# Two decode attentions in one kernel: the keys and values of the windowed one (A) loaded for all 16 heads at once, ahead of the other one's (B's) head pairs

## The chip, the cores and the metric

One NeuronCore of a Trainium2 chip runs the whole program. The metric is the device time of one execution in microseconds (us). Matmuls run on the tensor engine (PE; its weight loads are shown as PEld), elementwise work and reductions on the vector engine (DVE), exponentials on the scalar engine (ACT), set-up work on GpSimd (POOL), and loads are issued from the sync engine (SP) and carried out by 16 DMA engines.

## The reference

Two grouped-query attentions with one query token each. Every one has 32 query heads on 16 key heads of 128 elements, a cache of 8,192 tokens, a query projection and an output projection. A looks at the last W = 2,048 tokens only, B at all 8,192.

```python
Hq, Hkv, Sk, Dh, D = 32, 16, 8192, 128, 576
q = (x @ wq).reshape(1, 1, 32, 128).transpose(0, 2, 1, 3)
k = repeat(k_cache[:, :, Sk - W:, :], 2, axis=1)      # A: W = 2048; B: the whole cache
v = repeat(v_cache[:, :, Sk - W:, :], 2, axis=1)
scores = einsum("bhqd,bhkd->bhqk", q, k) * Dh ** -0.5
o = einsum("bhqk,bhkd->bhqd", softmax(scores), v)
out = o.transpose(0, 2, 1, 3).reshape(1, 1, 4096) @ wo
return concatenate([out_A, out_B], axis=-1)
```

All tensors are bfloat16. K and V are 4.2 MB per pair of B's heads, 8.4 MB for all of A's heads; wq and wo are 4.7 MB each. Together some 102.8 MB are read once.

## The kernel before

The program is written out by hand: each engine has a list of operations, and `op` and `load` put semaphore waits in front of an operation for the names in its `deps`. Within an engine the order of the list is the order of execution.

**Loads.** All big loads are issued from SP, in one list, into one buffer `ring` of 72 K elements (144 KB) per partition. `place` gives each load the next stretch, goes back to the start when it does not fit, and makes the load wait until the last use of what it overwrites (the names in `uses`). The order is wq of A and B, then for each of the eight head pairs p: K of B (4 MB, one row of 32 KB for each of 128 partitions), K of A (1 MB, two rows of 4 KB for each partition, one for each head), V of B, V of A; then wo of A, and wo of B in six pieces that get smaller.

**Queries.** x is spread over the partitions (`xd`, `xT`, `xr`), multiplied with wq in 16 units of 512 columns (`qmm`), copied out by ACT and DVE in turn (`qe`), transposed (`qT`), and laid into mostly zero weight blocks `zb` (B) and `za` (A), so that one 128-column matmul puts the two queries' scores of one slab of keys on their own rows of the score bank.

**A head pair.** K comes in slabs of 2,048 elements per partition: eight of B and two of A (`NI` = 10). DVE transposes a slab (L335, names `T`), PE multiplies it in four matmuls (L345, `S`), all ten into one bank. Then one softmax for B and A of this pair: maximum (`max`, L354), across partitions by a matmul (`mT`), per head on one partition (`mrB`, `mrA`, `mxB`, `mxA`), back to all partitions (`bc`, `nb`), exponential with row sums on ACT (`exp`, L380), two DVE transposes (`PT`, L384). The V matmuls follow (L393 for B, L400 for A, names `V`), the results are copied out (`xo0` on ACT, `xo1` on DVE, L409) and folded per head by PE (`OB` L414, `OA` L421). Scores alternate between two banks, three transposed slabs are kept (`NKT`).

**End.** Sums are inverted and applied (`lsel`, `L`, `rl`, `on`), the 32 heads are brought into wo's order (`oq`, `pm`, `oP`), and PE runs the output projection (L457, `F0.0`, then `F1.0` to `F1.5` as the pieces of wo land).

POOL makes an identity at the start and sets `zb`, `za`, `pts` to zero; DVE sets `vb` to zero and derives small selection tables from the identity.

Of the kernel before, what the change touches and what calls it, by code (L numbers as in the profile page):

```python
# [4 lines left out]
BF16 = mybir.dt.bfloat16  # L5
F32 = mybir.dt.float32
# [5 lines left out]
HQ = 32  # L12
# [9 lines left out]
NB = 2 * SK // 128 * DH // SLAB  # L22
NI = NB + 2
W0 = 2 * (NB - 1)
ZW = 128 + W0
RING = 72 * 1024
# [80 lines left out]
def bass_concat_heads__sliding_block_cached__gqa_block_cached__decode_kernel(nc, A_x, A_k_cache, A_v_cache, A_wq, A_wo,  # L107
# [5 lines left out]

    ring = nc.alloc_sbuf_tensor("ring", [128, RING], BF16)
# [12 lines left out]
    za = nc.alloc_sbuf_tensor("za", [128, NP, 2, 4, 128], BF16)  # L127
    mx = nc.alloc_sbuf_tensor("mx", [128, 2], F32)
    mr = nc.alloc_sbuf_tensor("mr", [128, 8], F32)
    mexp = nc.alloc_sbuf_tensor("mexp", [128, 128], F32)  # L130
    nb = nc.alloc_sbuf_tensor("nb", [128, 2], F32)
# [4 lines left out]
    cls = nc.alloc_sbuf_tensor("cls", [128, 8], F32)  # L136
    selb = nc.alloc_sbuf_tensor("selb", [128, 16], F32)
    sela = nc.alloc_sbuf_tensor("sela", [128, 4], F32)
    par = nc.alloc_sbuf_tensor("par", [128, 2], F32)
    lsel = nc.alloc_sbuf_tensor("lsel", [128, NP, 8], F32)  # L140
    rl = nc.alloc_sbuf_tensor("rl", [128, NP * 8], F32)
# [60 lines left out]
    kv_at = {}  # L202
    for p in range(NP):
        for kind, c in (("K", ks), ("V", vs)):
            use = "T%d.%d" if kind == "K" else "V%d.%d"
            src = c[1][0, 2 * p:2 * p + 2, :, :].rearrange("h (q t) d -> (h q) (t d)", q=64)
            kv_at[kind, p, 0] = place(NB * SLAB, [use % (p, NB - 1)],
                                      lambda e, t, src=src: e.dma_start(t, src), "%sB%d" % (kind, p))
            src = c[0][0, 2 * p:2 * p + 2, SK - W_A:SK, :].rearrange("h (q t) d -> q h (t d)", q=128)
            kv_at[kind, p, 1] = place(2 * SLAB, [use % (p, NI - 1)],  # L210
                                      lambda e, t, src=src: e.dma_start(t.rearrange("q (h n) -> q h n", h=2), src),
                                      "%sA%d" % (kind, p))
# [23 lines left out]
    op("pool", lambda e: e.memset(zb[:], 0.0), name="zb0")  # L236
    op("pool", lambda e: e.memset(za[:], 0.0), name="za0")
    op("pool", lambda e: e.memset(mexp[:], 0.0), name="mexp0")
    op("pool", lambda e: e.memset(onesf[:], 1.0), name="ones")
    op("pool", lambda e: e.memset(pts[:], 0.0), name="pts0")  # L240
# [3 lines left out]
    for b in range(2):  # L244
        op("dve", lambda e, b=b: e.memset(vb[b][:, :], 0.0), name="vb0.%d" % b)
# [3 lines left out]
    for h in range(2):  # L249
        op("dve", lambda e, h=h: e.tensor_reduce(  # L250
            cls[:, 2 * h:2 * h + 2], view(identf, 128, 64 * h, [[1, 2], [32, 2], [2, NB]]), AX.XY, ALU.add),
            deps=["identf"], name="clsB%d" % h)
    op("dve", lambda e: e.tensor_reduce(cls[:, 4:8], view(identf, 128, 2 * NB, [[1, 4], [32, 4]]), AX.X, ALU.add),
       deps=["identf"], name="clsA")
    op("dve", lambda e: e.tensor_reduce(selb[:], view(identf, 128, 0, [[1, 16], [32, 4]]), AX.X, ALU.add),
       deps=["identf"], name="selb")
    op("dve", lambda e: e.tensor_reduce(sela[:], view(identf, 128, 0, [[4, 2], [1, 2], [32, 4], [2, 2]]), AX.XY, ALU.add),
       deps=["identf"], name="sela")
# [3 lines left out]
    for P in range(2):  # L262
# [14 lines left out]
        for c in range(2):  # L277
            op("dve", lambda e, P=P, c=c: e.tensor_scalar(  # L278
                xrep[:, P, 4 + c, :], banks[2 * P + 1][:, 0:128], par[:, c:c + 1], None, ALU.mult),
                deps=["xT%d.4" % P, "par%d" % c], name="xr%d.%d" % (P, 1 + c))  # L280
    XR = ["xr%d.%d" % (P, c) for P in range(2) for c in range(3)]

    KT = NKT * SLAB
    for P in range(2):
        for n in range(8):
# [17 lines left out]
            else:  # L303
# [4 lines left out]
                deps=["qe%d" % u] + (["z0.%d" % i for i in range(8)] if P else []), name="qT%d" % u)  # L308
        srcs = [[512, NP], [64, 2], [1, 2], [128, 2]]
        for b in range(4):  # L310
            if P == 1:
                op("dve", lambda e, b=b: e.tensor_copy(
                    view(zb, NP * 4 * ZW, 32 * b + W0, [[4 * ZW, NP], [2 * ZW, 2], [ZW, 2], [1, 2]], 32, 32 * b),
                    view(ktb, KT, b // 2 * 256, srcs, 32, 32 * b)),
                    deps=["qT%d" % u for u in range(8, 16)] + ["zb0"], name="z1.%d" % b)
            else:
                for h in range(2):
                    op("dve", lambda e, b=b, h=h: e.tensor_copy(
                        view(za, NP * 1024, h * 512 + 32 * b + 2 * (NB + h),
                             [[1024, NP], [256, 2], [128, 2], [1, 2]], 32, 32 * b),  # L320
                        view(ktb, KT, h * 256, srcs, 32, 32 * b)),
                        deps=["qT%d" % u for u in range(8)] + ["za0"], name="z0.%d" % (2 * b + h))
    Z = ["z0.%d" % i for i in range(8)] + ["z1.%d" % i for i in range(4)]


    def unit(kind, p, s):
        return "%s%s%d" % (kind, "BA"[s // NB], p)

    for p in range(NP):
        for s in range(NI):  # L330
            k = p * NI + s
            kt = ktb[:, (k % NKT) * SLAB:(k % NKT + 1) * SLAB]
            deps = [unit("K", p, s)]
            deps += ["S%d" % (k - NKT)] if k >= NKT else Z
            op("dve", lambda e, p=p, s=s, kt=kt: e.transpose(kt.bitcast(I32), slab("K", p, s).bitcast(I32)),  # L335
               deps=deps, name="T%d.%d" % (p, s))

            def mm(e, p=p, s=s, k=k):
                for c in range(2):
                    for v in range(2):  # L340
                        if s < NB:
                            lhsT = zb[:, p, 2 * c + v, W0 - 2 * s:W0 - 2 * s + 128]
                        else:
                            lhsT = za[:, p, s - NB, 2 * c + v, :]
                        ins = e.matmul(sb[p % 2][:, :], lhsT=lhsT,  # L345
                                       rhs=view(ktb, KT, (k % NKT) * SLAB + 64 * c + v, [[128, 16], [2, 32]]),
                                       start=(s == 0 and c == 0 and v == 0), stop=(s == NI - 1 and c == 1 and v == 1))
                return ins
            deps = ["T%d.%d" % (p, s)]
            if s == 0:  # L350
                deps += ["exp%d" % (p - 2), "max%d" % (p - 2)] if p >= 2 else Z + ["qe%d" % u for u in range(16)]
            op("pe", mm, deps=deps, name="S%d" % k)

        op("dve", lambda e, p=p: e.tensor_reduce(mx[:, 0:1], sb[p % 2][:, :], AX.X, ALU.max),  # L354
           deps=["S%d" % (p * NI + NI - 1)] + (["mT%d" % (p - 1)] if p else []), name="max%d" % p)
        op("pe", lambda e: e.matmul(mb[0:1, 0:128], lhsT=mx[:, 0:1], rhs=identf[:, :], start=True, stop=True),  # L356
           deps=["max%d" % p, "identf"] + (["mrA%d" % (p - 1), "mrB1.%d" % (p - 1), "nb%d" % (p - 1)] if p else []),
           name="mT%d" % p)
        deps = ["mT%d" % p] + (["bc%d" % (p - 1)] if p else ["mexp0"])
        for h in range(2):  # L360
            op("dve", lambda e, h=h: e.tensor_reduce(
                mr[0:1, 2 * h:2 * h + 2], view(mb, 512, 64 * h, [[1, 2], [32, 2], [2, NB]], parts=1), AX.XY, ALU.max),
                deps=deps + (["mxB%d.%d" % (h, p - 1)] if p else []), name="mrB%d.%d" % (h, p))
        op("dve", lambda e: e.tensor_reduce(
            mr[0:1, 4:8], view(mb, 512, 2 * NB, [[1, 4], [32, 4]], parts=1), AX.X, ALU.max),
            deps=deps + (["mxA%d" % (p - 1)] if p else []), name="mrA%d" % p)
        for h in range(2):
            op("dve", lambda e, h=h: e.tensor_scalar(
                view(mexp, 128, 64 * h, [[32, 2], [2, NB], [1, 2]], parts=1),
                view(mr, 8, 2 * h, [[0, 2], [0, NB], [1, 2]], parts=1), -SCALE, None, ALU.mult),  # L370
                deps=["mrB%d.%d" % (h, p)], name="mxB%d.%d" % (h, p))
        op("dve", lambda e: e.tensor_scalar(
            view(mexp, 128, 2 * NB, [[32, 4], [1, 4]], parts=1),
            view(mr, 8, 4, [[0, 4], [1, 4]], parts=1), -SCALE, None, ALU.mult),
            deps=["mrA%d" % p], name="mxA%d" % p)
        op("pe", lambda e: e.matmul(mb[:, 128:129], lhsT=mexp[0:1, :], rhs=onesf[0:1, 0:1], start=True, stop=True),
           deps=["mxA%d" % p, "mxB0.%d" % p, "mxB1.%d" % p, "ones"], name="bc%d" % p)
# [5 lines left out]
        for h in range(2):  # L383
            op("dve", lambda e, h=h: e.transpose(  # L384
                view(pts, 1024, 2 * h, [[4, 16], [64, 16], [1, 2]], 64, 64 * h), psb[64 * h:64 * h + 64, :]),
               deps=["exp%d" % p] + (["V%d.%d" % (p - 1, NI - 1)] if p else ["pts0"]), name="PT%d.%d" % (h, p))

        for s in range(NI):
            def mm(e, p=p, s=s):
                src = slab("V", p, s)  # L390
                if s < NB:
                    for j in range(4):
                        ins = e.matmul(vb[0][32 * j:32 * j + 16, :],  # L393
                                       lhsT=view(pts, 1024, 64 * s + 16 * j, [[1, 16]]),
                                       rhs=src[:, 512 * j:512 * j + 512], start=(s == 0), stop=(s == NB - 1))
                else:
                    h = s - NB
                    for t in range(8):
                        j = t % 4
                        ins = e.matmul(vb[1][32 * j:32 * j + 8, 256 * h:256 * h + 256],  # L400
# [104 lines left out]
```

## Time and profile before

Three runs took 249.95, 250.19 and 251.74 us; the median is 250.19. One execution was profiled.

| what | value |
|---|---|
| the profiled execution: its time, its span | 250.0 us, 248.2 us |
| bytes read, mean rate over the span | 102.76 MB, 414 GB/s |
| DMA engines, share of the span in the SP queue's packets | 97.9% |
| PE busy, DVE busy, ACT busy, POOL busy | 73%, 62%, 7%, 5% |
| granted PE clock, mean | 0.82 |
| DVE transposes of K slabs (L335) | 80, 92.4 us, 1,213 ns each |
| score matmuls (L345) | 320, 90.3 us |
| loads of K and V of B: size, issue to landing | 4,096 KB, 27 us |
| loads of K and V of A: size, issue to landing | 1,024 KB, 27 to 29 us |

The span runs from the first to the last instruction of the profile; the 1.8 us around it belong to the time. The "busy" of an engine is the time in which it has an instruction in work. A DMA packet is one contiguous row as a DMA engine moves it. "Issue to landing" is how long after SP issued a load its data were complete, waiting behind earlier loads included.

### The profile page before, as it was taken

The numbers are of one execution on the slowest core, as the hardware profiler recorded it, in microseconds if no ns is written. First come the engines' busy times: TensorE is split into PE (matmuls) and PEld (weight loads), VectorE is DVE, ScalarE is ACT, GpSimd is POOL, SyncE is SP. The second block draws the span as 40 slices with busy tenths as digits, with TensorE's granted clock in tenths as the row PEclk, the third lists the DMA queues.
The fourth block names the chain that finished last, engine by engine and source line by source line (L and its number), as shares of the span: only waits on it lengthen the run. The fifth ranks groups of instructions, "written<-read, shape, count | busy, mean of one in ns | idle before, by whom it ended". The sixth has DMA issues, their size and how long they took to land.

```text
span 248.2 us, 2581 instructions
## 1 busy us (share of the span) xinstructions
PE 181.7 (73%) x1085; PEld 80.7 (33%) x1085; DVE 153.1 (62%) x228; ACT 18.1 (7%) x36; POOL 13.4 (5%) x15
## 2 busy tenths in 40 slices
PE   0039994957995799379746984998489757975795
PEld 0013441313631342143224321732153124322552
DVE  8963779952885298439734873487349725972300
ACT  2001220010001000100010001000100010001000
POOL 8920000000000000000000000000000000000000
PEclk9999999795589599877987597569677957895769
DMA  7999999999999999999999999999999999999992
GB/s 264 418 490 433 422 422 416 417 428 418 427 414 434 419 458 419 436 432 431 421 429 414 434 422 428 420 422 419 433 420 433 428 433 422 436 403 457 395 406 111
DMA packets 8262, 102.92 MB, mean 415 GB/s; under 512 B 694, under 2 KB 956, under 8 KB 5564
## 3 DMA queue, kind: packets, MB, share of 16 engines
q1 hardware_dynamic: 8248, 102.77, 97.9%
q8 instruction: 8, 0.13, 0.2%
q14 instruction: 2, 0.02, 0.0%
q10 hardware_dynamic: 4, 0.00, 0.0%
HBM read 102.76 MB, written 0.00 MB: 414 GB/s over the span
## 4 chain that ended last, share of the span: by engine, by line
DMA 32%; DVE 31%; PE 30%; issue 3%; ACT 2%; SPq 0%; POOL 0%; POOLq 0%; DVEq 0%
DMA ring<-in_B_k_cache_dram 22%; DVE ktb L335 18%; DMA ring<-in_B_wo_dram 10%; PE sb L345 10%; PE vb L393 7%; DVE xdup L263 5%; PE sb L295 4%; PE qb L295 3%; DVE pts L384 3%; ACT psb L380 2%; PE ob L414 1%; DVE mx L354 1%; PE ob L421 1%; PE vb L400 1%; PE mb L356 1%
## 5 line engine op out<-in xcount | busy, mean ns | idle before, releaser
L335 DVE STREAM_TRANSPOSE ktb<-ring 128x1024 int32<-128x1024 int32 x80 | 92.4, 1213 | 11.3 <-DMA ring<-in_B_k_cache_dram 7.6
L345 PE MATMUL sb<-ktb,zb 128*128 128x512 bf16 x256 | 73.6, 443 | 11.0 <-DVE ktb L335 9.8
L345 PEld LDWEIGHTS sb<-ktb,zb 128*128 128x128 bf16 x256 | 25.6, 110 | 56.3 <-DVE ktb L335 24.2
L393 PE MATMUL vb<-ring,pts 128*16 128x512 bf16 x256 | 28.2, 619 | 21.1 <-DVE pts L384 21.1
L409 DVE COPY xo<-vb 128x512 f32<-128x512 f32 x8 | 5.5, 692 | 35.8 <-PE vb L400 35.8
L393 PEld LDWEIGHTS vb<-ring,pts 128*16 128x16 bf16 x256 | 8.5, 123 | 34.3 <-issue 34.2
L345 PE MATMUL sb<-ktb,za 128*128 128x512 bf16 x64 | 16.7, 381 | 1.3
L380 ACT ACTIVATE psb<-sb,nb 128x512 bf16<-128x512 f32 x8 | 5.5, 687 | 140.9 <-DVE nb L378 140.9
L384 DVE STREAM_TRANSPOSE pts<-psb 64x512 bf16<-64x512 bf16 x16 | 11.3, 706 | 7.0 <-ACT psb L380 6.8
L295 PE MATMUL sb<-ring,xrep 128*128 128x512 bf16 x40 | 11.2, 438 | 1.3 <-DVE xrep L278 1.3
L263 DVE COPY xdup<-xrow 1x128 bf16<-1x128 bf16 x2 | 11.3, 5660 | 0.0
L457 PE MATMUL qb<-ring,oP 128*1 128x288 bf16 x128 | 10.9, 346 | 0.5 <-DVE oP L446 0.4
L414 PEld LDWEIGHTS ob<-selb,xo 128*128 128x128 f32 x64 | 10.1, 242 | 3.4 <-ACT xo L407 3.4
L354 DVE TENSOR_REDUCE mx<-sb 128x1 f32<-128x512 f32 x8 | 5.5, 692 | 9.1 <-PE sb L345 9.1
L414 PE MATMUL ob<-selb,xo 128*128 128x4 f32 x64 | 10.8, 293 | 0.3 <-ACT xo L407 0.3
L272 PE MATMUL sb<-onesb,xrow 1*128 1x128 bf16 x4 | 0.6, 295 | 14.0 <-DVE xdup L263 14.0
L306 DVE STREAM_TRANSPOSE ktb<-qsb 128x256 int32<-128x256 int32 x16 | 7.0, 443 | 6.1 <-ACT qsb L301 5.8
L421 PE MATMUL ob<-sela,xo 128*128 128x2 f32 x64 | 9.9, 276 | 0.0
L421 PEld LDWEIGHTS ob<-sela,xo 128*128 128x128 f32 x64 | 9.5, 227 | 0.0
L295 PE MATMUL qb<-ring,xrep 128*128 128x512 bf16 x40 | 9.3, 379 | 0.0
L345 PEld LDWEIGHTS sb<-ktb,za 128*128 128x128 bf16 x64 | 4.9, 96 | 13.1 <-DVE ktb L335 9.2
L457 PEld LDWEIGHTS qb<-ring,oP 128*1 128x1 bf16 x128 | 6.1, 99 | 5.3 <-DMA ring<-in_B_wo_dram 1.2
(66 smaller groups left out, 83.0 us busy)
## 6 DMA issues: line engine op xcount, KB each, us to landing
ring<-in_B_k_cache_dram SPq DMA_DIRECT2D x8, 4096.0 KB, 27.0
ring<-in_B_v_cache_dram SPq DMA_DIRECT2D x8, 4096.0 KB, 26.8
ring<-in_A_k_cache_dram SPq DMA_DIRECT2D x8, 1024.0 KB, 28.9
ring<-in_A_v_cache_dram SPq DMA_DIRECT2D x8, 1024.0 KB, 27.2
ring<-in_A_wo_dram SPq DMA_DIRECT2D x1, 4608.0 KB, 28.2
ring<-in_A_wq_dram SPq DMA_DIRECT2D x1, 4096.0 KB, 12.2
ring<-in_B_wq_dram SPq DMA_DIRECT2D x1, 4096.0 KB, 22.3
ring<-in_B_wo_dram SPq DMA_DIRECT2D x1, 2304.0 KB, 33.4
```

Of the source, the lines that this page charges most:

```text
L263: op("dve", lambda e, P=P: e.tensor_copy(view(xdup, 256, 128 * P, [[2, 64], [1, 2]], parts=1), view(xrow, 2 * DM, P * DM + 512, [[1, 64], ...
L295: ins = e.matmul(bank[:, :], lhsT=lhsT, rhs=o, start=(k == 0), stop=(k == 4))
L306: op("dve", lambda e, n=n: e.transpose(ktb[:, n * 512:(n + 1) * 512].bitcast(I32), qsb[:, n % 2, :].bitcast(I32)), deps=["qe%d" % u] + ([" ...
L335: op("dve", lambda e, p=p, s=s, kt=kt: e.transpose(kt.bitcast(I32), slab("K", p, s).bitcast(I32)), deps=deps, name="T%d.%d" % (p, s))
L345: ins = e.matmul(sb[p % 2][:, :], lhsT=lhsT, rhs=view(ktb, KT, (k % NKT) * SLAB + 64 * c + v, [[128, 16], [2, 32]]), start=(s == 0 and c = ...
L354: op("dve", lambda e, p=p: e.tensor_reduce(mx[:, 0:1], sb[p % 2][:, :], AX.X, ALU.max), deps=["S%d" % (p * NI + NI - 1)] + (["mT%d" % (p - ...
L380: op("act", lambda e, p=p: e.activation(psb[:, :], sb[p % 2][:, :], ACT.Exp, bias=nb[:, p % 2:p % 2 + 1], scale=SCALE, accum_out=rsall[:, ...
L384: op("dve", lambda e, h=h: e.transpose(view(pts, 1024, 2 * h, [[4, 16], [64, 16], [1, 2]], 64, 64 * h), psb[64 * h:64 * h + 64, :]), deps= ...
L393: ins = e.matmul(vb[0][32 * j:32 * j + 16, :], lhsT=view(pts, 1024, 64 * s + 16 * j, [[1, 16]]), rhs=src[:, 512 * j:512 * j + 512], start= ...
L414: ins = e.matmul(ob[:, 8 * p:8 * p + 4], lhsT=xo[:, 0, 128 * t:128 * t + 128], rhs=selb[:, 4 * t:4 * t + 4], start=(t == 0), stop=(t == 3))
L421: ins = e.matmul(ob[:, 8 * p + 4 + 2 * h:8 * p + 6 + 2 * h], lhsT=xo[:, 1, 256 * h + 128 * t:256 * h + 128 * t + 128], rhs=sela[:, 2 * t:2 ...
L457: ins = e.matmul(fb[r:r + 1, 0:288], lhsT=oP[:, 1 - P, k0 + k:k0 + k + 1], rhs=wo_at[P, c][:, k * DM + 288 * n:k * DM + 288 * n + 288], st ...
```

## The change

A leaves the loop over pairs and comes ahead of it, for all 16 heads together. Each partition holds 256 consecutive tokens of one head: partition 8h + r has the r-th eighth of head h, so that A's K is 64 KB per partition and comes in two loads of 32 KB rows (4 MB each), and so does V. The source pattern has the 16 heads outermost. All four loads stand on SP's list between wq and B's first K.

```diff
 kv_at = {}
+for kind, c in (("K", ks[0]), ("V", vs[0])):
+    for i in range(NA // NB):
+        src = bass.AP(tensor=c.tensor, offset=c.offset + (SK - W_A) * DH + i * ROW,
+                      ap=[[SK * DH, G], [TA * DH, 128 // G], [1, ROW]])
+        kv_at[kind, "A", i] = place(ROW, [...], lambda e, t, src=src: e.dma_start(t, src), "%sA%d" % (kind, i))
 for p in range(NP):
...
-        src = c[0][0, 2 * p:2 * p + 2, SK - W_A:SK, :].rearrange("h (q t) d -> q h (t d)", q=128)
-        kv_at[kind, p, 1] = place(2 * SLAB, [use % (p, NI - 1)],
-                                  lambda e, t, src=src: e.dma_start(t.rearrange("q (h n) -> q h n", h=2), src),
-                                  "%sA%d" % (kind, p))
```

The sixteen slabs of A's keys fill four score banks (`sb` and `qb`). Since each partition holds one head's tokens, a matmul gives scores of all queries against all heads' keys; a matmul of two small tables (`mkl`, `mkr`) first writes a large negative number where head and group do not belong together. One softmax serves all heads of A, and one chain of 64 V matmuls with 128-column weights writes one bank:

```diff
+for g in range(4):
+    op("pe", lambda e, g=g: e.matmul(banks[g][:, :], lhsT=mkl..., rhs=mkr..., start=True, stop=False), ...)
+    for cc in range(4):
+        scores(4 * g + cc, ..., lambda ce, cc=cc: za[:, ce, ZA - 128 - 8 * cc:ZA - 8 * cc], banks[g], ...)
+    op("dve", ... tensor_reduce(mx[:, g:g + 1], banks[g][:, :], AX.X, ALU.max), name="maxA%d" % g)
+# maxA, mTA, mrA, mxA, bcA, nbA: once
+for g in range(4):
+    op("act", ... activation(psa[:, g % 2, :], banks[g][:, :], ACT.Exp, ...), name="expA%d" % g)
+    for b in range(4):
+        op("dve", ... transpose(view(pta, ...), psa[32 * b:32 * b + 32, g % 2, :]), name="PA%d.%d" % (g, b))
+for s in range(NA):                     # four matmuls each
+    ins = e.matmul(vb[1][:, :], lhsT=pta[:, 4 * i:4 * i + 4, :]..., rhs=src[:, 512 * j:512 * j + 512], ...)
+op("act", ... activation(xo[:, 1, :], vb[1][:, :], ACT.Copy), name="xoA")
+op("pe", fold_a, deps=["xoA", "identf"], name="OA")         # four matmuls, once
```

The loop over pairs keeps B alone: eight slabs, `mrB`/`mxB`, 32 V matmuls, `xo` on ACT, `OB`. The queries of A go into one `za` of 608 columns with four copies in place of eight. The zeroing of `za`, `zb` and `pts` moves from POOL to DVE, behind the spreading of x, together with that of the new `pta` (8,192 columns) and of `vb` and with the small tables. The columns of `ob`, `lsel`, `rl` and `on` are in the order A, B instead of pair by pair.

## Prediction

> **What bounds the kernel now.** I read the page's slices first, then its DMA queues and its chain, then the waits of SP's queue and of DVE, the table of windows, and last the groups.
>
> ```profile
> DMA  7999999999999999999999999999999999999992
> GB/s 264 418 490 433 422 422 416 417 428 418 427 414 434 419 458 419 436 432 431 421 429 414 434 422 428 420 422 419 433 420 433 428 433 422 436 403 457 395 406 111
> ...
> q1 hardware_dynamic: 8248, 102.77, 97.9%
> q8 instruction: 8, 0.13, 0.2%
> ...
> DMA 32%; DVE 31%; PE 30%; issue 3%; ACT 2%; SPq 0%; POOL 0%; POOLq 0%; DVEq 0%
> ```
>
> The sixteen DMA engines are busy in every slice but the first and the last. The chain of work (last line) shares the time out evenly and would mislead here: it follows compute that keeps pace with the loads. The windows (us, PE, PEld, DVE, ACT, POOL busy, clock, DMA share, GB/s) and SP's waits say which of the two sets the pace:
>
> ```profile
> 24.00:36.00 12.00, 12.00 (x57) 5.43 (x56) 9.87 (x25) 3.08 (x6) 0.00 (x0) 1.00 1.00 428
> 40.00:206.00 166.00, 129.13 (x741) 55.37 (x741) 104.88 (x146) 9.63 (x21) 0.00 (x0) 0.79 1.01 426
> ```
>
> ```profile
> SPq L208 <- DVE ktb L335: 55.0, 5, 12.0
> SPq L208 <- PE vb L393: 38.0, 4, 10.7
> ...
> SPq L211 <- PE qb L295: 24.7, 1, 24.7
> ```
>
> ```profile
> DVE ktb L335 <- DMA ring<-in_B_k_cache_dram: 7.6, 5, 2.2
> ```
>
> ```profile
> ring<-in_B_k_cache_dram SPq DMA_DIRECT2D x8, 4096.0 KB, 27.0
> ring<-in_B_v_cache_dram SPq DMA_DIRECT2D x8, 4096.0 KB, 26.8
> ring<-in_A_k_cache_dram SPq DMA_DIRECT2D x8, 1024.0 KB, 28.9
> ```
>
> SP waits for ring space, yet a 4 MB load lands 27 us after its issue while its own bytes need 9.8 us (4.19 MB at 427 GB/s). So some 17 us of other loads always stand ahead of it, and a late slab costs nothing until it is later than that. The loads set the end; what matters is time on the DMA engines, and whether the ring ever runs dry.
>
> The trace keeps a record of every packet and every landing. Grouped by size: 4,352 packets of 4,096 B took 162.7 ns on average, 2,304 of 32,768 B took 1,222.7 ns (26.8 B/ns per engine). Each load raises its semaphore by sixteen single increments, and those of K of B's pair 0 come between 34.42 and 34.91 us: sixteen equal shares, 0.5 us apart at most.
>
> **The change, part by part.** *Packets.* Removed: 4,096 packets of 4 KB (16 loads x 128 partitions x 2 heads), 4,096 x 162.7 ns / 16 engines = 41.7 us. Added: 512 of 32 KB (4 loads x 128 rows). At the row of B's 32 KB packets they cost 512 x 1,222.7 / 16 = 39.1 us, a gain of 2.5 us. That twelve loads fewer are issued saves 12 sixteen-fold increments of 9.3 ns, 0.1 us, and each issue on SP (0.4 us) was hidden in the 17 us.
>
> What the trace does not show is the new address pattern. Every K, V, wq and wo load of before has 128 outer rows on both sides. The new A loads have 16 heads outermost in HBM (2 MB apart, 8 rows of 64 KB pitch in each) and 128 partitions in SBUF. If the sixteen equal shares follow the heads, engine e writes the eight neighbouring partitions 8e to 8e+7, and which engines write to the same part of SBUF at the same time changes. The lower bound of a packet is B's row, 1,222.7 ns. The upper bound is that each engine shares its way with one other all the time: the way's capacity is what one engine fills (busy share 1.00, no idle time to give), so a packet takes 2 x 1,222.7 = 2,445 ns. The nearest row for sharing is q8: instruction fetches run beside q1 on the same engines, and their 16,384 B packets took 1,091 ns, 15.0 B/ns, 1.78 times B's time per byte. Three prices for A's loads: 39.1, 69.6 (x1.78) and 78.2 us (x2). I take x2, as two equal streams that start within 0.5 us of each other and alternate have no unequal partner, unlike a fetch: 78.2 - 41.7 = **+36.6 us**.
>
> [...]
>
> *A's compute, now in front.* DVE:
>
> ```profile
> L335 DVE STREAM_TRANSPOSE ktb<-ring 128x1024 int32<-128x1024 int32 x80 | 92.4, 1213 | 11.3 <-DMA ring<-in_B_k_cache_dram 7.6
> L345 PE MATMUL sb<-ktb,zb 128*128 128x512 bf16 x256 | 73.6, 443 | 11.0 <-DVE ktb L335 9.8
> L384 DVE STREAM_TRANSPOSE pts<-psb 64x512 bf16<-64x512 bf16 x16 | 11.3, 706 | 7.0 <-ACT psb L380 6.8
> L409 DVE COPY xo<-vb 128x512 f32<-128x512 f32 x8 | 5.5, 692 | 35.8 <-PE vb L400 35.8
> ```
>
> Sixteen transposes of A's slabs (16 x 1.21 = 19.4 us) are moved, not added. Added: 16 transposes PA (half of L384's partitions, so at most 0.71 each, 11.3) and four maxima (2.8); removed: eight xo copies (5.5) and mrA/mxA (2.5). PE: 64 V matmuls of full width at 0.216 (L295: 10 in 2.16 us) to 0.443, 14 to 28 us, replace 7.8 of L400; L421's 64 fold matmuls become 8. In the forecast the loads hide it all: wq ends at 25.2 us, K of A lands at 44.8 and 64.3, V at 83.9 and 103.4, B's first K at 113.2. Scores of A end near 76, exp and PA near 91, V near 111 (8 slabs x 4 x 0.216 after 103.4) to 118. PE's queue holds pair 0's scores behind V of A, so pair 0 starts up to 5 us late and the ring absorbs it: K of pair 1 needs VA7 (near 92; due 123), V of pair 1 VA15 (118; due 133). Per pair the loads take 19.6 us; compute loses two slabs (2.4), L400 (0.85) and OA (1.0 to 1.8) from the 22.6 to 25.3 that lie between the V starts of neighbouring pairs in the timeline, waits for loads included, which leaves 18.3 to 20.9: it keeps up.
>
> *Start.* The memsets of za, zb and pts leave POOL (6.9, 3.9 and 1.0 us), and xdup, which took 11.1 us beside them, ends earlier. DVE gets 14,368 columns of memsets, 13.6 us by L245 (0.95 ns a column); q's evictions stand behind them. Both end before K of A has landed at 44.8: nothing. If K lands at 35 (no sharing), the old 39.7 still holds within 2 us, and the 17 us of loads ahead cover that.
>
> *Tail.* K of the last pair used to be followed by 36.9 us of loads (landing 208.5, last 245.4); without A's K and V behind it, by 31.9. Compute after that landing takes, by the rows of pair 7: scores 10.7, softmax 4.75, V 3.4, copy 0.9, fold 1.05, normalising 2.25, so F (L457) starts at 23.05 instead of 26.15. F0 took 6.96 and F1's first 48 matmuls 2.1 (64: 2.8): end at 32.8. The last matmuls trail the landing by 0.3 now, so this is 32.8 - 31.9 - 0.3 = +0.6 (0 with F0 as fast as F1; +4.7 with F1 as slow as F0).
>
> **Sum** against the profiled execution (span 248.2, time 250.0): 250.0 + 36.6 - 0.1 + 0.6 = 287.1. [...] I say 287.0.
>
> **Rivals.** *A's rows ride like B's* (the shares are dealt out by partitions as before; not slower): 250.0 - 2.6 + 0.6 = 248.0, and 247.4 if the tail costs nothing. For it: same 32 KB rows, same 128 partitions. Against: the outermost count is 16. It decides if A's packets stay under 1.3 us. [...] *The front starves the ring* without any sharing: V of A done at 78 to 94 us, V of pair 1 due at 92, pair 0's V at 98 to 119, due 111: 0 to 8 us, so 248.0 to 256; the cover is the 17 us. That the change doesn't do what it says is excluded for the order of the loads: SP's queue is written out.
>
> **How the numbers follow.** Sharing throughout (278 to 292) 0.64; drift 0.14; like B's 0.13; starved front 0.05; dearer than 294 0.04. The range 258 to 294 holds the first and most of the second. A measurement of this kernel tells about 1% from no change, 2.5 us. Slower: 0.64 + 0.14 + 0.04 + 0.03 = 0.85. Like B's lies at -0.8%, so its 0.13 and the rest of the front split into faster 0.07 and same 0.08.
>
> **What would show it.** Right: 32 KB packets near 2.4 us between 25 and 103 us, GB/s in the slices there near 215 at a full busy share, and about 425 from then on; DVE waiting for K of A. Wrong: GB/s flat at 425 (like B's), rising within the phase (drift), or DMA idle slices between 80 and 120 us (front).

## The result: 290.2 us, 1.16 times the time before

| | before | after |
|---|---|---|
| median (lowest to highest), four runs each | 250.07 us (249.83 to 251.74) | 290.22 us (289.15 to 292.49) |
| the profiled execution: time, span | 250.0, 248.2 us | 291.08, 289.0 us |
| DMA engines, share of the span in the SP queue's packets | 97.9% | 97.4% |
| mean rate over the span | 414 GB/s | 356 GB/s |

The ratio of the times is 1.160 (95% interval 1.151 to 1.169): slower, by 40 us. The forecast was 287.0 in a range of 258 to 294. Where runs of one kernel fall into fast and slow ones, a ratio here is that of the fast ones and a median that of all.

The page of after, its slices first (40 equal ones, 7.2 us each), then the line of its DMA queue, the chain by engine and three rows of loads (size, us from issue to landing):

```profile
DMA  7999999999999999999999999999999999999991
GB/s 291 435 435 290 218 217 218 218 218 213 213 218 195 209 313 420 431 422 426 422 435 433 435 435 433 435 431 431 432 429 435 435 426 435 424 425 445 411 394 60
...
q1 hardware_dynamic: 4472, 102.76, 97.4%
...
DMA 46%; DVE 23%; PE 18%; another core or an unknown queue 9%; ACT 1%; issue 1%; SPq 1%
...
ring<-in_B_k_cache_dram SPq DMA_DIRECT2D x8, 4096.0 KB, 29.6
...
ring<-in_A_k_cache_dram SPq DMA_DIRECT2D x2, 4096.0 KB, 53.8
ring<-in_A_v_cache_dram SPq DMA_DIRECT2D x2, 4096.0 KB, 66.8
```

The DMA engines never stop, but from the fourth slice to the fifteenth they move half as much. Read alone, the busy line would show nothing; it has to be read with the line under it. The table of windows (us, PE, PEld, DVE, ACT, POOL busy, clock, DMA share, GB/s) puts borders on it:

```profile
3.00:25.00 22.00, 11.62 (x50) 4.87 (x47) 15.61 (x30) 2.41 (x5) 0.00 (x0) 1.00 1.05 429
25.00:44.00 19.00, 9.18 (x41) 3.92 (x41) 8.77 (x22) 2.39 (x4) 0.00 (x0) 0.85 0.95 198
44.00:64.00 20.00, 10.19 (x34) 3.27 (x34) 10.54 (x10) 0.00 (x0) 0.00 (x0) 0.76 1.03 216
64.00:84.00 20.00, 10.94 (x37) 3.60 (x37) 11.79 (x15) 1.25 (x4) 0.00 (x0) 0.76 1.01 213
84.00:104.00 20.00, 8.41 (x32) 3.38 (x32) 10.81 (x16) 1.75 (x6) 0.00 (x0) 0.76 1.01 215
...
125.00:206.00 81.00, 60.07 (x314) 23.74 (x312) 49.70 (x68) 5.50 (x12) 0.00 (x0) 0.79 1.01 433
```

Every one of A's four loads runs at about half rate, from its first row to its last: A's landings stand 19.8 to 20.0 us apart, 211 GB/s for 4.19 MB. B's loads are back at full rate. The packet records say the same: A's 512 packets of 32 KB took 2,486 ns on average, B's 1,217 to 1,222, load by load, after B's first K (1,316, as some of its packets ran beside A's last ones). Compute waits (us in total, times, longest us):

```profile
DVE ktb L347 <- DMA ring<-in_B_k_cache_dram: 51.7, 8, 21.4
DVE ktb L347 <- DMA ring<-in_A_k_cache_dram: 16.2, 2, 10.1
```

Where the 41.1 us between the two profiled executions lie: the last load lands at 284.68 us in place of 245.42 (+39.3), the last matmul ends 1.8 us after it in place of about 0.4 (+1.4), and the stretch from there to the end of the time grew by 0.4.

### The profile page after: what moved, and what is told of

Its sections match the earlier page's. It is cut to its first block, busy times and chain, and to the rows that moved or that the text cites. A ratio compares the mean times of both kernels' runs of the same rounds, so it can differ in the third digit from the quotient of the medians.

```text
span 289.0 us, 2344 instructions
## 1 busy us (share of the span) xinstructions
PE 186.2 (64%) x973; PEld 76.1 (26%) x973; DVE 156.9 (54%) x231; ACT 21.7 (7%) x45; POOL 1.8 (1%) x12
## 3 DMA queue, kind: packets, MB, share of 16 engines
q1 hardware_dynamic: 4472, 102.76, 97.4%
## 4 chain that ended last, share of the span: by engine, by line
DMA 46%; DVE 23%; PE 18%; another core or an unknown queue 9%; ACT 1%; issue 1%; SPq 1%
DMA ring<-in_B_k_cache_dram 31%; DMA ring<-in_A_k_cache_dram 15%; DVE ktb L347 15%; PE sb L353 8%; DVE pta L389 4%; PE qb L492 3%; PE vb L446 3%; PE qb L353 2%; PE ob L456 1%; DVE pts L438 1%; DVE mx L368 1%; ACT psb L434 1%; DVE mx L416 0%; ACT xo L451 0%
## 5 line engine op out<-in xcount | busy, mean ns | idle before, releaser
L347 DVE STREAM_TRANSPOSE ktb<-ring 128x1024 int32<-128x1024 int32 x80 | 92.6, 1214 | 70.1 <-DMA ring<-in_B_k_cache_dram 51.7
L353 PE MATMUL sb<-ktb,zb 128*128 128x512 bf16 x256 | 71.6, 427 | 4.5 <-DVE ktb L347 2.5
L397 PE MATMUL vb<-ring,pta 128*128 128x512 bf16 x64 | 17.1, 434 | 15.7 <-DMA ring<-in_A_v_cache_dram 15.7
L353 PE MATMUL sb<-ktb,za 128*128 128x512 bf16 x32 | 9.6, 444 | 14.2 <-DVE ktb L347 14.0
L353 PE MATMUL qb<-ktb,za 128*128 128x512 bf16 x32 | 9.9, 455 | 9.7 <-DVE ktb L347 9.4
L397 PEld LDWEIGHTS vb<-ring,pta 128*128 128x128 bf16 x64 | 6.8, 109 | 25.6 <-DMA ring<-in_A_v_cache_dram 16.3
L389 DVE STREAM_TRANSPOSE pta<-psa 32x512 bf16<-32x512 bf16 x16 | 11.2, 703 | 1.3 <-ACT psa L385 0.8
L492 PE MATMUL qb<-ring,oP 128*1 128x288 bf16 x128 | 9.0, 317 | 0.4 <-DVE oP L481 0.4
L353 PEld LDWEIGHTS sb<-ktb,za 128*128 128x128 bf16 x32 | 3.1, 109 | 20.3 <-DVE ktb L347 16.6
L451 ACT ACTIVATE xo<-vb 128x512 f32<-128x512 f32 x8 | 4.8, 597 | 40.7 <-PE vb L446 40.7
L315 PEld LDWEIGHTS sb<-ring,xrep 128*128 128x128 bf16 x40 | 4.1, 107 | 13.0 <-issue 9.7
## 6 DMA issues: line engine op xcount, KB each, us to landing
ring<-in_A_v_cache_dram SPq DMA_DIRECT2D x2, 4096.0 KB, 66.8
```

The source lines that it names most:

```text
L315: ins = e.matmul(bank[:, :], lhsT=lhsT, rhs=o, start=(k == 0), stop=(k == 4))
L347: op("dve", lambda e: e.transpose(kt.bitcast(I32), src.bitcast(I32)), deps=[kind] + (["S%d" % (k - NKT)] if k >= NKT else Z), name=name)
L353: ins = e.matmul(bank[:, :], lhsT=lhsT(2 * c + v), rhs=view(ktb, KT, (k % NKT) * SLAB + 64 * c + v, [[128, 16], [2, 32]]), start=(start an ...
L389: op("dve", lambda e, g=g, b=b: e.transpose(view(pta, TA * 32, 64 * 32 * g + 8 * b, [[32, 16], [512, 4], [1, 8]], 32, 32 * b), psa[32 * b: ...
L397: ins = e.matmul(vb[1][:, :], lhsT=pta[:, 4 * i:4 * i + 4, :].rearrange("p t k -> p (t k)"), rhs=src[:, 512 * j:512 * j + 512], start=(i = ...
L492: ins = e.matmul(fb[r:r + 1, 0:288], lhsT=oP[:, P, k0 + k:k0 + k + 1], rhs=wo_at[P, c][:, k * DM + 288 * n:k * DM + 288 * n + 288], start= ...
```

## The experiments

Two questions. Is it the address pattern of A's loads that costs 40 us, and what in it: the distances in HBM, the outermost count, or the partitions that are written together? And would the change have paid without that cost? Where no number of runs is named, a time is that of one run.

**A's rows flat, other keys.** The source of A's loads becomes the first 128 rows of the cache in a row; place, size and packets stay.

```diff
-            src = bass.AP(tensor=c.tensor, offset=c.offset + (SK - W_A) * DH + i * ROW,
-                          ap=[[SK * DH, G], [TA * DH, 128 // G], [1, ROW]])
+            src = bass.AP(tensor=c.tensor, offset=c.offset + i * 128 * ROW, ap=[[ROW, 128], [1, ROW]])
```

> The changed kernel, with A's four loads reading 128 consecutive 32 KB rows each (the first 8 MB of A's caches, so other keys than the last 2,048 of each head). Bytes, packets, order, destinations and all compute stay. Theory S (the sixteen heads as the outermost count of the source give each DMA engine eight neighbouring partitions, and two engines share a way into SBUF): the packets of A return to 1.22 us and the time to 248.0 us, 247.4 to 251 with the tail's bounds. Rival H (the addresses in HBM are slow: heads 2 MB apart, rows 64 KB apart): the same 248, since these addresses are as flat as B's. Rival F (A's compute in front starves the ring): packets at 1.22 us and still 255 us or more, with DMA idle between 80 and 120 us. So this run separates F from the other two, and measures what the rest of the change is worth.

Measured: 255.03 us (median of 10; ratio to before 1.0128, interval 1.0078 to 1.0178). A's 32 KB packets are back at 1,214 to 1,225 ns, load by load. So the pattern accounts for 35 of the 40 us; but the time is not the 248 of theory S.

```profile
DMA  8899999999999999999999999999999999999940
GB/s 311 379 471 415 430 459 427 420 420 425 462 430 420 417 430 456 425 425 420 441 443 425 425 417 446 441 425 420 424 446 430 430 425 425 388 420 388 413 165 0
...
PE 52%; DVE 34%; DMA 5%; ACT 5%; issue 3%; SPq 0%; DVEq 0%
```

The loads are done at 244.32 us, 1.1 us sooner than in the kernel before, and the last slice has no traffic: now compute ends last. The ten runs agree with that: they took 251.5 us at a granted PE clock of 0.86 and 257.8 at 0.82, while eleven of thirteen runs of the kernel before took 249.8 to 250.2 at any clock from 0.813 to 0.835. The trace shows where compute fell behind. These are lines of PE's timeline (start, us busy): V of A, the scores of pair 0 and of pair 7, the output projection.

```profile
71.39 16.46 PE L396 MATMUL vb<-ring,pta 128*128 128x512 bf16 x62 [4.47 <-DVE pta L388]
...
89.45 7.92 PE L352 MATMUL sb<-ktb,zb 128*128 128x512 bf16 x32
...
220.44 9.20 PE L352 MATMUL sb<-ktb,zb 128*128 128x512 bf16 x32
...
241.56 8.75 PE L491 MATMUL qb<-ring,oP 128*1 128x288 bf16 x128 [0.41 <-DVE oP L480]
```

V of A runs on PE from 71.4 to 87.9 us, with pair 0's scores queued behind it: they start at 89.3 with their first weight load, though their keys landed at 75.0. That is a lag of 14 us. The pairs then follow each other every 18.7 us (89.34 to 220.23 for seven), and their keys land every 19.5 (75.00 to 211.53), so only 0.8 us of it is won back per pair; at pair 7 it is still 9 us (keys at 211.5, scores at 220.2), and the output projection, which starts at 241.6, ends at 250.3.

**Sixteen outermost, near addresses.** Blocks of eight neighbouring rows, 16 blocks, within 4.6 MB (other keys again).

```diff
+            pitch = 8 * ROW + 16384
+            src = bass.AP(tensor=c.tensor, offset=c.offset + i * G * pitch, ap=[[pitch, G], [ROW, 8], [1, ROW]])
```

> As the flat-rows run, but the source is written as 16 groups of 8 rows of 32 KB, the groups 288 KB apart instead of 256 KB, so that the outermost count is 16 again and no address is 2 MB from another one in step (it reads other keys). Theory S: A's packets near 2.45 us and the time near 290 us, as in the changed kernel. Rival H: 1.22 us and 248 us.

Measured: 290.37 us, A's packets 2,505 ns on average. The distance between addresses is not the cause.

**128 outermost, far addresses.** The counterpart: a pitch of 256 KB, 128 rows outermost (other keys).

```diff
+            src = bass.AP(tensor=c.tensor, offset=c.offset + i * ROW, ap=[[SK * DH // 8, 128], [1, ROW]])
```

> As the changed kernel, but the source has 128 rows outermost at one pitch of 256 KB, so that rows of neighbouring heads are still 2 MB apart, while the outermost count is 128 on both sides (it reads other keys of each head). Theory S: A's packets near 1.22 us, 248 us. Rival H: as slow as the changed kernel or slower, 2.4 us and 290 us.

Measured: 255.6 us, A's packets 1,214 to 1,225 ns, load by load. Together the two runs part the addresses from the outermost count: of the two it is the count that matters.

**The same pattern in the kernel before.** K of B's pairs 2 to 5 (other keys) get 16 outermost rows; all else, A's place included, is as before.

```diff
+            if kind == "K" and 2 <= p < 6:
+                src = bass.AP(tensor=c[1].tensor, offset=c[1].offset + 2 * p * SK * DH,
+                              ap=[[8 * NB * SLAB + 2048, 16], [NB * SLAB, 8], [1, NB * SLAB]])
```

> The kernel before, with the K loads of B's pairs 2 to 5 (16.8 MB, as many bytes as A has) read as 16 groups of 8 rows of 32 KB, the groups 4 KB further apart than they are long (so up to 240 of a head's keys shifted). Nothing is moved to the front. Theory S: these four loads take 19.6 us each in place of 9.8, so 250.0 + 4 x 9.8 = 289 us. Rivals H and F: 250 us, as the addresses are nearly consecutive and no compute is moved.

Measured: 301.88 us. Its slices:

```profile
GB/s 315 446 428 419 419 423 432 403 466 362 212 210 259 431 340 206 212 276 431 292 211 200 322 412 287 213 193 351 412 458 419 418 441 411 432 440 413 414 269 20
```

Four stretches near 210 GB/s, one for each of the four loads, so the pattern costs as much in B and in the middle of the kernel. But 51.9 us more, where 39 were expected. The 32 KB packets make 40.6 of it (2,304 packets, mean 1,504 ns in place of 1,223, over 16 engines). The 4 KB packets make 6.5: some 700 of them, on engines that were already in the next load, took 311 ns on average in place of 163, so a slow load slowed down its neighbours too. And the engines came apart, which is about the remaining 4.7: the 2.3 us between the first and the last of the sixteen increments of the last load became 7.0.

**Rows in another order.** Each of A's loads becomes eight loads of 16 rows (row r of all 16 heads), in the order 0, 4, 1, 5, 2, 6, 3, 7.

```diff
+            def issue(e, lo, j, c=c, i=i):
+                r = ORDER[j]          # 0, 4, 1, 5, 2, 6, 3, 7
+                src = bass.AP(tensor=c.tensor, offset=c.offset + (SK - W_A) * DH + r * TA * DH + i * ROW,
+                              ap=[[SK * DH, G], [1, ROW]])
+                return e.dma_start(bass.AP(tensor=ring, offset=r * RING + lo, ap=[[8 * RING, G], [1, ROW]]), src)
```

> The changed kernel with each of A's four loads cut into eight loads of one row per head (16 rows of 32 KB, partitions r, 8 + r, 16 + r, ...), all from SP, in the order r = 0, 4, 1, 5, 2, 6, 3, 7. [...] With the 0.3 to 1.0 us by which engines were apart in the changed kernel's A phase, packets fall from 2.47 to between 1.5 and 2.2 us, and the time to between 258 and 282 us. Rival R (an engine that reads a head of its own is slow at the source, whatever it writes): packets stay at 2.47 us, 290 us.

Measured: 284.77 us, packets 2,297 ns on average in the first load and 2,331 to 2,335 in the others, there nearly the same for every engine and every row. Neither theory S (258 to 282 us) nor rival R (290 us) holds: another order of the rows is worth 5 us, and the rate stays near half.

**The same with a lag for some engines.** Two small loads ahead of A's (12 rows and 4 rows of 8 KB) should set engines apart.

```diff
+    for m, (rows, part) in enumerate(((12, 16), (4, 0))):
+        load("sp", lambda e, rows=rows, part=part: e.dma_start(
+            bass.AP(tensor=ring, offset=part * RING + RING - 4096, ap=[[RING, rows], [1, 4096]]), ...
```

> [...] Theory S: partners no longer meet, packets near 1.22 us, 255 us (the flat rows' time), up to 2.4 us more for the late engines. Rival R: 290 us and more.

Measured: 283.22 us, packets 2,306 ns on average in the first load and 2,198 to 2,200 in the others, for all sixteen engines. The lag came only in part (the 8 KB packets took about 455 ns, and some engines stood 1.2 to 1.7 us apart), so for theory S, in which partners no longer meet, this is a weak test. What it does show: engines that no longer run in step still have equal packets.

**Two queues.** Rows 0 to 3 of each load are issued from SP, rows 4 to 7 from ACT, so that two loads are in work at once.

```diff
+                load("sp", ...)                      # rows 0 to 3
+            late.append((fn, s_ld[n % NSEM], given)) # rows 4 to 7, from ACT's list
```

> [...] Theory S, if an engine takes packets of its two queues in turn: both ways of a pair are in use most of the time, packets at 1.3 to 2 us, 255 to 275 us; if it drains the queues in step with its partner, nothing is gained and packets stay at 2.45 us, 290 us. Rival R: 290 us.

Measured: 286.45 us, packets 2,300 to 2,355 ns, load by load. From its third packet on each engine takes a row of the one queue and a row of the other in turn, so the order is again an alternating one, and the rate is that of the alternating rows from one queue (2,297 to 2,335 ns): the second queue frees nothing more. The two ways of a pair that theory S speaks of no run shows.

**Other partitions.** Loads of 16 rows as above, from the same addresses; only the partitions change, from load to load.

```diff
+PARTS = {"near": lambda r: (16 * r, [[1, 16]]),                                      # first K of A
+         "seven": lambda r: (r, [[7, 16]]) if r < 7 else (112, [[1, 16]]),           # second K
+         "four": lambda r: (64 * (r // 4) + r % 4, [[4, 16]]),                       # first V
+         "eight": lambda r: (r, [[8, 16]])}                                          # second V
```

> Only the partitions that A's rows are written to are changed (A's values then stand in other partitions); each of A's four loads is again eight loads of 16 rows, row r of all 16 heads, from the same addresses as in the changed kernel. First K: heads in neighbouring partitions (16r + h). Second K: seven partitions apart (7h + r; its last 16 rows in neighbouring ones). First V: four apart. Second V: eight apart, as in the rows-alternate run. Theory P (what counts is which partitions are written at the same time, in groups of four partitions: neighbours share the most): packets of the first K about 4,900 ns (four engines to a group), of the second K 1,222 to 2,445, of both V about 2,330; 300 to 306 us. Rival C (a load with 16 rows outermost goes at half rate wherever its rows are written): 2,310 to 2,330 ns in all four loads, 285 us.

Measured: 304.17 us, within what theory P gave. Its slices, then windows inside the first K, the second K, the first and the second V:

```profile
GB/s 326 430 425 208 130 121 107 169 278 195 187 213 200 208 208 282 436 438 434 421 434 447 423 430 421 432 443 430 425 435 436 430 425 425 430 440 418 425 404 57
```

```profile
27.00:60.00 33.00, 9.18 (x41) 3.93 (x41) 7.46 (x18) 2.39 (x4) 0.00 (x0) 0.68 0.99 129
62.00:72.00 10.00, 8.21 (x26) 2.69 (x25) 7.32 (x8) 0.00 (x0) 0.00 (x0) 0.78 1.08 282
79.00:98.00 19.00, 10.76 (x37) 3.62 (x37) 13.64 (x19) 1.50 (x5) 0.00 (x0) 0.77 0.98 200
100.00:114.00 14.00, 8.38 (x30) 3.26 (x28) 6.44 (x10) 0.78 (x2) 0.00 (x0) 0.74 0.98 204
```

Four kinds of loads, all with 16 outermost rows and the same sources, at different rates: packets of 4,230 to 4,260 ns where 16 neighbouring partitions are written, 2,290 to 2,550 at steps of four and eight. At steps of seven the rate changes from row to row: medians of 2,020 to 2,120 ns in rows 1, 2, 5 and 6, but 1,580 and 1,640 in rows 3 and 4 (row 0 still runs beside the load before, and the last row, to neighbouring partitions, took 3,830). The rival, half rate whatever the partitions, is out. Which partitions are written at the same time decides. The first K is dear, though not the 4,900 of theory P, and its range for the steps of seven was not one of fast and slow engines side by side: nearly all sixteen are slower or faster together, row by row.

**Is the lag V of A's?** The flat-rows kernel with one in four of A's V matmuls.

```diff
-            for j in range(4):
+            for j in range(1):
```

> The flat-rows kernel with one of four V matmuls of A left out three times in four (16 in place of 64; A's output then lacks most of its tokens). Theory L (the flat-rows kernel is slower than before because PE's 64 V matmuls of A, 16.5 us, stand ahead of pair 0's scores, and the pairs win only 0.7 us each of that back): pair 0's scores start within 2 us of the landing of its keys, DMA engines set the end again, last matmul 2 us after the last landing: 249 to 251 us. Rival (the pairs without A's slabs are themselves too slow for the loads): the pairs fall behind again, 253 to 255 us.

Measured (one run): 250.0 us, span 248.1; the flat-rows kernel's profiled execution took 254.85, and the one run of the kernel before beside this one 252.05. Pair 0's scores start at 83.4 us in place of 89.3. That is still 8 us behind their keys (75.3), not the 2 expected: DVE's transposes of the exponentials hold up what is left of V (the groups start 2.5 to 3.0 us apart, each at the release of its transposes), and the scores stand behind them.

```profile
73.43 1.89 PE L396 MATMUL vb<-ring,pta 128*128 128x512 bf16 x4 [0.98 <-DVE pta L388]
76.45 1.87 PE L396 MATMUL vb<-ring,pta 128*128 128x512 bf16 x4 [1.14 <-DVE pta L388]
79.30 1.89 PE L396 MATMUL vb<-ring,pta 128*128 128x512 bf16 x4 [0.98 <-DVE pta L388]
```

Of the timeline's columns the first is the start, the second the busy time, the bracket the wait. At pair 7 the lag is 3.2 us, the last load lands at 243.43 and the last matmul ends at 245.62. So 6 us less in front are 5.4 less at pair 7 and 4.85 less at the end: the front's compute does reach the end, nearly one for one. Some 6 of the 14 us are the left-out matmuls; the rest, by this timeline, is the softmax chain ahead of them (no run leaves that out).

**A in front, in the pattern of before.** A's four loads are as early and as large, with 128 rows outermost and eight heads of 4 KB in each.

```diff
+            src = c[0, 8 * i:8 * i + 8, SK - W_A:SK, :].rearrange("h (q t) d -> q h (t d)", q=128)
```

> A's loads are as large and as early as in the changed kernel (four of 4 MB ahead of B's), and read A's own keys and values, but in the address pattern of the kernel before: 128 rows outermost, eight heads in each, packets of 4 KB (the layout in a partition is then one that A's tables do not fit). Theory P (the dealing of rows to engines and partitions costs 39 us, the earlier place of A's loads nothing on the DMA engines): 4,096 packets near 157 ns, A's loads 40 to 42 us, GB/s near 420 in every slice; then the lag of the flat-rows kernel decides: 253 to 257 us. Rival (large loads of A in front are slow in themselves, by their heads 2 MB apart): GB/s near 215 in the front slices, 285 us or more.

Measured: 253.75 us (median of four runs, 251.67 to 257.69; ratio 1.0123, interval 1.0052 to 1.0194). The windows of A's loads and of the pairs behind them:

```profile
25.00:66.00 41.00, 28.86 (x114) 10.05 (x112) 31.69 (x48) 3.84 (x9) 0.00 (x0) 0.96 1.04 415
70.00:206.00 136.00, 106.59 (x528) 44.22 (x528) 83.30 (x109) 9.62 (x21) 0.00 (x0) 0.75 1.00 431
```

A's own bytes, heads 2 MB apart, early and in 4 MB loads, at 415 GB/s. What is left, 1.2%, is the lag: in the profiled execution (257.69 us, the slowest of the four) pair 0's scores start 9.0 us after their keys have landed, and the last matmul ends 7.0 us after the last load.

## Why the prediction came out right, and where not

**The bound: right.** The loads set the end before and after; the DMA line stays at 9 and the chain of after goes to the DMA engines (46% of the span in place of 32%).

**The packets: right in kind, a little small.** The step took twice B's row, 2,445 ns; measured 2,486. That is 1.3 us more over 512 packets and 16 engines, so the term is +37.9 in place of +36.6. B's first K, beside A's last packets, adds 0.8 (128 packets at 1,316 ns in place of 1,217), a term that the sum did not have. Of the 39.3 us by which the last load landed later, some 0.6 stay unplaced. The choice between the three prices was the whole forecast: at q8's 1.78 it would have been 278, at B's row 248. That two engines share a way, from which the factor of two comes, no run shows, and twice B's row was no upper bound either: A's packets took 1,214 to 1,225 ns from flat rows, 2,486 in this pattern and 4,230 to 4,260 into 16 neighbouring partitions.

**Its reason: the place confirmed, the picture not.** That the cost comes from which partitions are written together is shown: near addresses do not cure it (2,505 ns a packet), far ones do not cause it (1,214 to 1,225), other partitions, with the same sources, move it between 1,580 and 4,260 ns. But the prediction had partner engines sharing one way in pairs, each pair by itself. Then some pairs should come apart and have short packets at times, and engines with partitions of their own should keep full speed. Neither was seen. In after itself the packets of all sixteen engines have the same length at the same time: of the 369 of A's packets that start after 46 us, 277 take 2,520 to 2,550 ns, 68, on most engines every fourth, 2,320 to 2,350, and 22 lie between these (2,351 to 2,472). In the alternating order all have 2,331. The limit in these loads is common to the sixteen. So the factor of two was right for these partitions, but that it came out within 2% is in part luck: it was worked out from a picture that does not hold. Nor does a small group of neighbouring partitions make up a way: at steps of four and of eight no two rows of a load lie in the same four partitions, and they still cost double (2,290 to 2,550 ns). What the way is physically, and how a load's rows are dealt to the engines, no run shows directly; and as engines stand up to 2.8 us apart in the run with other partitions, the figures of its neighbouring rows mix.

**The rival "drift": not borne out.** The rate does not rise within the phase (198, 216, 213, 215 GB/s).

**The rival "like B's": mispriced.** It gave 248.0 if A's packets were B's. They were, in the flat-rows kernel, and it took 255.0. The step that failed is "the ring absorbs it": a ring that never runs dry keeps the loads going (true: a DMA share of 0.98 to 1.01 in the flat-rows kernel's windows between 25 and 206 us), but it does not bring late compute back. The prediction had the pairs keep up (18.3 to 20.9 us of compute against 19.6 of loads); 18.7 against 19.5 does keep up, and wins back only 0.8 us per pair. A lag of 14 us in front is still 9 at the tail. The rival "starved front" had a range to 256 and so the right size, for a wrong reason: the DMA engines did not starve.

**A's compute in front: hidden, as said, in the kernel as it is.** K of A landed at 46.9 and 66.8 us (predicted 44.8, 64.3), V at 86.6 and 106.6 (83.9, 103.4), B's first K at 116.6 (113.2): all late by the dearer packets. The last score matmuls of A start at 79.8 (76 said), its last transpose ends at 95.3 (91), V is done at 115.3 (111 to 118), and pair 0 starts 1.3 us after its keys. The slow loads are the cover: at full rate the same work is the lag.

**Start: right.** The q matmuls start at 14.3 us in place of 18.1, and the last query transpose starts at 35.5 us, well before K of A is there.

**Tail: +1.4 in place of +0.6**, inside its bounds (0 to +4.7).

## What to carry to other kernels

Before giving a load a new address pattern, work out which partitions its rows reach at the same time; a pattern with 16 rows outermost over 128 partitions cost a factor of two here (2,486 and 2,505 ns a packet against 1,214 to 1,225), with the DMA engines busy in every slice, and all four kernels that kept 128 rows outermost for these loads read them at 415 GB/s or more. Read GB/s beside the busy line, always. And work brought ahead of a steady pipeline is paid at the end unless the pipeline has slack per turn: divide the lag by what one turn wins (here 14 us by 0.8, some 18 turns, where the kernel has eight) before calling it absorbed.

## What the runs showed of the hardware that was not expected

- All sixteen engines' packets had one length at one time in these loads, in step (2,331 ns in the alternating order) or 1.2 to 1.7 us apart (2,198 to 2,200 with the lag). When an instruction fetch held one engine near 42 us, all engines' packets got shorter at once: 2,541 to about 2,500 ns in after, 2,314 to 2,289 in the alternating order.
- A slow load slowed down others in work beside it: in the kernel before with 16 outermost rows, 4 KB packets took 311 ns on average beside it in place of 163, and in after the 32 KB packets of B's first K 1,316 in place of 1,217.
- Engines that came apart stayed apart: the sixteen increments of a load lie 2.0 us apart at 46.9 us in after and still 2.2 at the last load, and 7.0 us apart at the end of the kernel before with four such loads.
